# Ordering TensorE's queue by hand in an Infini-attention plus SiLU kernel: an emission clock, held-back dependent work, w1 products spread over the score tiles

## The chip, the cores and the metric

The kernel runs on one core of one Trainium2 chip. The metric is device time in microseconds (us), lower is better. Engines are named as the profile names them: PE is the matrix engine (TensorE), ACT the scalar engine, DVE the vector engine, POOL the GpSimd engine, SP the queue that issues most DMAs.

## The reference, cut to what matters

```python
xn  = layernorm(x)                       # x: 2048 rows x 512
out = x + attention(xn) + mlp(xn)

# attention: 32 heads of 16, four segments of 512 rows, one after another
q, k, v = xn @ wq, xn @ wk, xn @ wv
for s in range(4):
    p     = softmax(qs @ ks.T / 4 + causal_mask)
    a_dot = p @ vs
    a_mem = (phi(qs) @ M) / (phi(qs) @ z + 1e-6)
    o_s   = g * a_mem + (1 - g) * a_dot          # g = sigmoid(beta), per head
    M, z  = M + phi(ks).T @ vs, z + sum(phi(ks)) # phi(t) = t + 1 if t > 0 else exp(t)
attention = concat(o_s) @ wo

# mlp: 512 -> 1792 -> 512
mlp = silu(xn @ w1) @ w2
```

## The kernel before

The work of a segment is cut into 20 score tiles. A score tile is four or eight small matmuls into four PSUM banks, one exp of 128x2048 on ACT, and a causal mask on POOL. All else on PE is "filler" put between score tiles: the next segment's projections, PV and Z (the softmax's denominators), the memory matrix (`psM`), normalisation (`psR`, `psD`, `psN`), 14 w1 products per segment (`ps`, then tanh on ACT, a product on DVE, giving one `hT` tile), and four output rows per segment with 14 w2 and 4 wo matmuls each. All fillers share three PSUM banks (`pp`), but for Z, which adds up in a bank of its own.

The program's text fixes the order only roughly. The scheduler of the framework, which works with a model of durations, orders every engine's queue, PE's too. The main loop hands out fillers by a budget:

```python
    def fillers(s):
        # ... (segment 0: rest of the projections, layernorm of segment 1)
        if s > 0 and s < 3:
            yield from mem_fill(s, sts[s], sts[s + 1])
        if s < 3:
            # ...
            yield from proj_fill(s + 1, sts[s + 1])
        if s > 0:
            yield from out_fill(s - 1, sts[s - 1])   # normalise, w2, wo of the last segment
        yield from h_some(s, FT)                     # 14 w1 products in a row
        # ...

            for quad in range(5):
                s_quad(st, dt, quad, tiles)          # scores, exp, mask
                budget += STEP_BUDGET                # 2300
                # ...
                while budget > 0:
                    c = next(fill, None)
                    if c is None:
                        break
                    budget -= c
```

One w1 product shows the dependent chain that matters: PE, then ACT, then DVE, and only then is the PSUM bank free again (the page of the kernel before puts 4.7 us of PE's waits at this line on that DVE product).

```python
            ps = gemm4(...)                                           # PE, 4 matmuls
            nc.scalar.activation(out=th[:], in_=ps[:, :], func=AF.Tanh)
            nc.vector.scalar_tensor_tensor(                           # (tanh + 1) * ps
                out=hT[:], in0=th[:], scalar=1.0, in1=ps[:, :], op0=ALU.add, op1=ALU.mult)
```

Tanh gives silu because w1 is scaled by 0.5 first, which is a job of POOL in the head of the program.

The softmax here doesn't subtract the row's maximum and nothing guards it: scores larger than these inputs give would overflow.

Of the kernel before, what the change touches and what calls it, by code (L numbers as in the profile page):

```python
# [1 line left out]

# [9 lines left out]
F32 = mybir.dt.float32  # L12

P = 128
# [13 lines left out]
STEP_BUDGET = 2300  # L28
# [3 lines left out]
def kernel(  # L32
# [20 lines left out]
    hpool = ctx.enter_context(tc.tile_pool(name="hpool", bufs=20))  # L53
# [4 lines left out]
    psatt = ctx.enter_context(tc.tile_pool(name="psatt", bufs=1, space=bass.MemoryType.PSUM))  # L58


    beta_b = cpool.tile([P, H], BF16, name="beta_b")
    nc.gpsimd.dma_start(
        out=beta_b[:], in_=bass.AP(tensor=A_beta.tensor, offset=A_beta.offset, ap=[[0, P], [1, H]])
    )
# [6 lines left out]

    xts = {}

    def load_x(s, half, eng):
        xt = xpool.tile([P, 2, D], BF16, name="x_in")
        r0 = s * L + half * 256
        eng.dma_start(
            out=xt[:], in_=x_flat[r0 : r0 + 256, :].rearrange("(two p) d -> p two d", p=P)
        )
        xts[(s, 2 * half)] = xt[:, 0, :]  # L80
        xts[(s, 2 * half + 1)] = xt[:, 1, :]

    load_x(0, 0, nc.sync)
    load_x(0, 1, nc.scalar)
    nc.sync.dma_start(out=wk_sb[:], in_=A_wk.rearrange("(ko ki) n -> ki ko n", ki=P))
    nc.scalar.dma_start(out=wq_sb[:], in_=A_wq.rearrange("(ko ki) n -> ki ko n", ki=P))
    nc.sync.dma_start(out=wv_sb[:], in_=A_wv.rearrange("(ko ki) n -> ki ko n", ki=P))
    nc.sync.dma_start(out=w1_sb[:], in_=B_w1.rearrange("(ko ki) n -> ki ko n", ki=P))
    nc.sync.dma_start(out=wo_sb[:], in_=A_wo.rearrange("(ko ki) n -> ki ko n", ki=P))
    nc.sync.dma_start(out=w2_sb[:], in_=B_w2.rearrange("(ko ki) n -> ki ko n", ki=P))  # L90
    load_x(1, 0, nc.scalar)
    load_x(1, 1, nc.sync)

# [3 lines left out]

# [7 lines left out]
    oneh = cpool.tile([P, 8, 32], BF16, name="oneh")  # L105
    nc.gpsimd.memset(oneh[:], 0.0)
    for i in range(8):
        nc.gpsimd.memset(oneh[:, i, i : i + 1], 1.0)


    zbias = cpool.tile([P, 1], F32, name="zbias")
    nc.gpsimd.memset(zbias[:], 1.0)
    for g in range(4):
        nc.gpsimd.memset(zbias[32 * g : 32 * g + 16, :], 1e-6)
        nc.gpsimd.memset(zbias[32 * g : 32 * g + 8, :], 0.0)


    smask = cpool.tile([P, H], F32, name="smask")
    nc.gpsimd.memset(smask[:], 0.0)
    for base, val in ((0, -1.0), (8, 1.0)):  # L120
        for dt in range(DT):
            v = smask[:, 8 * dt : 8 * dt + 8].rearrange("p (b c) -> p b c", b=4)
            nc.gpsimd.affine_select(
                out=v, in_=v, compare_op=ALU.not_equal, fill=val, base=-(base + 2 * dt),
                pattern=[[-32, 4], [-1, 2]], channel_multiplier=1,
            )
    gt = cpool.tile([P, H], F32, name="gt")
    gcol = cpool.tile([P, 1], F32, name="gcol")
    nc.vector.tensor_tensor(out=gt[:], in0=smask[:], in1=beta_b[:], op=ALU.mult)
    nc.vector.reduce_sum(out=gcol[:], in_=gt[:], axis=mybir.AxisListType.X)  # L130
    nc.scalar.activation(out=gcol[:], in_=gcol[:], func=AF.Tanh, scale=0.5)
    nc.vector.tensor_scalar(
        out=gcol[:], in0=gcol[:], scalar1=0.5, scalar2=0.5, op0=ALU.mult, op1=ALU.add
    )
    selb = cpool.tile([P, 2, DT, 8], F32, name="selb")
    nc.gpsimd.memset(selb[:], 0.0)
    for w, base in ((0, 0), (1, 8)):
        for dt in range(DT):
            v = selb[:, w, dt, :].rearrange("p (a b) -> p a b", a=4)
            nc.gpsimd.affine_select(  # L140
                out=v, in_=v, compare_op=ALU.not_equal, fill=1.0, base=-(base + 2 * dt),
                pattern=[[-32, 4], [-1, 2]], channel_multiplier=1,
            )
    sel = cpool.tile([P, 2, DT, P], BF16, name="sel")
    nc.vector.tensor_scalar(
        out=sel[:, :, :, :].rearrange("p w t (h d) -> p (w t h) d", d=DH),
        in0=selb[:, :, :, :].rearrange("p w t h -> p (w t h)").unsqueeze(2).broadcast_to([P, 64, DH]),
        scalar1=gcol[:, 0:1], scalar2=None, op0=ALU.mult,
    )


    bmask = cpool.tile([P, P], BF16, name="bmask")
    zmask = cpool.tile([P, DT, P], BF16, name="zmask")
    nc.gpsimd.memset(bmask[:], 1.0)
    nc.gpsimd.memset(zmask[:], 0.0)
    bm_v = bmask[:, :].rearrange("p (a b) -> p a b", a=8)
    for v in [bm_v]:
        nc.gpsimd.affine_select(
            out=v, in_=v, compare_op=ALU.is_ge, fill=0.0, base=0,
            pattern=[[-16, 8], [0, 16]], channel_multiplier=1,  # L160
        )
        nc.gpsimd.affine_select(
            out=v, in_=v, compare_op=ALU.is_ge, fill=0.0, base=15,
            pattern=[[16, 8], [0, 16]], channel_multiplier=-1,
        )
    for dt in range(DT):
        zv = zmask[:, dt, :].rearrange("p (g r) -> p g r", g=4)[:, :, 8 + 2 * dt : 10 + 2 * dt]
        nc.gpsimd.tensor_copy(
            out=zv, in_=bm_v[:, :, 0].rearrange("p (g r) -> p g r", g=4)
        )  # L170
# [6 lines left out]
    lnc = cpool.tile([P, TPS, 2], F32, name="lnc")  # L177
    nc.gpsimd.memset(lnc[:, :, 0:1], EPS)
    nc.gpsimd.memset(lnc[:, :, 1:2], -0.5)

    def ln_stats(s):
        for j in range(TPS):
            t = s * TPS + j
            stats = work.tile([P, nc.vector.BN_STATS_DIM], F32, name="stats")
            nc.vector.bn_stats(out=stats[:], in_=xts[(s, j)])
            nc.vector.bn_aggr(out=mv_all[:, t, :], in_=stats[:])
        rs = rstd_all[:, s * TPS : (s + 1) * TPS, :]
        nc.gpsimd.tensor_tensor(
            out=rs, in0=mv_all[:, s * TPS : (s + 1) * TPS, 1:2], in1=lnc[:, :, 0:1], op=ALU.add
        )  # L190
        nc.gpsimd.tensor_tensor(out=rs, in0=rs, in1=lnc[:, :, 1:2], op=ALU.pow)

    def ln_tile(s, j):
        t = s * TPS + j
        xn_t = work.tile([P, D], BF16, name="xn_t")
        nc.vector.tensor_scalar(  # L196
            out=xn_t[:], in0=xts[(s, j)],
            scalar1=mv_all[:, t, 0:1], scalar2=rstd_all[:, t, 0:1],
            op0=ALU.subtract, op1=ALU.mult,
        )  # L200
        ptr = pp.tile([P, 4, P], BF16, name="ptr", tag="ps")
        for dt in range(DT):
            nc.tensor.transpose(ptr[:, dt, :], xn_t[:, dt * P : (dt + 1) * P], ident[:])  # L203
        nc.vector.tensor_copy(out=xnT[s][:, :, j * P : (j + 1) * P], in_=ptr[:, :, :])

    def ln_fill(s):
        ln_stats(s)
        xnT[s] = segp.tile([P, DT, L], BF16, name="xnT")
        yield 0
        for j in range(TPS):  # L210
            ln_tile(s, j)
            yield 280


    def gemm4(lhsTs, rhss):
        ps = pp.tile([P, L], F32, name="ps", tag="ps")
        for ki in range(DT):
            nc.tensor.matmul(  # L218
                ps[:, :], lhsT=lhsTs(ki), rhs=rhss(ki), start=(ki == 0), stop=(ki == DT - 1)
            )  # L220
        return ps

    def phi_part(ps, dst, acc=None):
        ek = work.tile([P, L], BF16, name="ek", bufs=2)
        nc.scalar.activation(out=ek[:], in_=ps[:, :], func=AF.Exp)  # L225
        nc.gpsimd.tensor_scalar(  # L226
            out=ek[:], in0=ek[:], scalar1=1.0, scalar2=0.0, op0=ALU.min, op1=ALU.max
        )
        nc.vector.scalar_tensor_tensor(  # L229
            out=dst, in0=ps[:, :], scalar=0.0, in1=ek[:], op0=ALU.max, op1=ALU.add, accum_out=acc  # L230
        )

    vts = []
    for i in range(2):
        vt = cpool.tile([P, TPS, H // 2, 3, DH], BF16, name=f"V{i}")
        nc.gpsimd.memset(vt[:, :, :, 1, :], 0.0)
        vts.append(vt)

    def proj_fill(s, st):
        kT = segp.tile([P, DT, L], BF16, name="kT")  # L240
        kTo = segp.tile([P, DT, L], BF16, name="kTo")
        qT = segp.tile([P, DT, L], BF16, name="qT")
        V = vts[s % 2]
        st.update(kT=kT, kTo=kTo, qT=qT, V=V)
        if s < NSEG - 1:
            phiK = segp.tile([P, TPS, D], BF16, name="phiK", bufs=1)
            zc = segp.tile([P, DT], F32, name="zc")
            st.update(phiK=phiK, zc=zc)
        if s > 0:
            phiQT = segp.tile([P, DT, L], BF16, name="phiQT", bufs=3)  # L250
            st["phiQT"] = phiQT

        pend = []

        def k_transposes(dt, phiKT):
# [107 lines left out]
    def out_fill(s, st):  # L363
        while "rec" not in st:
            yield None
# [256 lines left out]
```

## Time and profile before

The kernel before takes 353.62 us (median of three runs, 351.61 to 354.32). The profiled execution has a span of 349.9 us.

| what | before |
|---|---|
| first scores on PE | 24.0 us |
| exp of the first / 80th score tile starts | 25.1 / 309.4 us |
| mean distance of two exps | 3.60 us |
| from the 80th exp's start to the end | 40.5 us |

These lines of the profile's page of the kernel before give the busy time of each engine, then PE's busy share and the granted PE clock in 40 slices of the span (a digit is tenths; 9 is 90% or more):

```profile
PE 276.9 (79%) x2416; PEld 120.5 (34%) x2452; DVE 176.4 (50%) x308; ACT 195.0 (56%) x166; POOL 131.7 (38%) x251
...
PE   0388868898987899998799789978589997642696
...
PEclk9999999999997899999999999999959999755599
```

No engine is full. PE is nearest, and at the end of the program (slices 35 to 38) it is both half idle and at half clock. The same page has the largest group of ACT, the exps: after the bar stand their busy time and mean duration in ns, then how long ACT was idle just before them and for whom it waited.

```profile
L446 ACT ACTIVATE Pt<-psS 128x2048 bf16<-128x2048 f32 x80 | 150.2, 1877 | 70.2 <-PE psS L439 69.8
```

ACT waited 70 us in all for score tiles: exps do not follow one another every 1.88 us, PE's order decides when each may start. The next view is the windows view of the kernel before. A line is a stretch, its length, then the busy time of PE, PE's weight loads, DVE, ACT and POOL in it, the granted clock, DMA share and GB/s. The first three are head, body and tail.

```profile
0.00:24.02 24.02, 8.30 (x32) 3.48 (x33) 11.18 (x30) 2.68 (x4) 18.65 (x69) 1.00 0.96 305
24.02:309.40 285.38, 243.73 (x2262) 106.60 (x2297) 150.75 (x262) 189.75 (x160) 111.47 (x182) 0.96 0.05 15
309.40:349.90 40.50, 24.85 (x122) 10.42 (x123) 14.52 (x18) 2.56 (x2) 1.60 (x2) 0.71 0.06 20
...
40.00:60.00 20.00, 15.42 (x141) 7.23 (x147) 17.32 (x43) 10.44 (x12) 14.14 (x28) 1.00 0.08 27
310.00:320.00 10.00, 3.34 (x41) 1.88 (x42) 4.04 (x2) 1.96 (x2) 1.09 (x1) 0.50 0.00 0
```

The body has 41.6 us without PE work, the tail 15.7, the head 15.7. (Some matmul records are missing from this trace: PE has 2416 beside 2452 weight loads, so busy times of PE are a little low. The tail's 122 should be 124.) Last, the timeline of the kernel before in its head; a line is start, duration, engine, source line, operation, and in brackets how long the engine was idle before it and what released it.

```profile
8.94 1.29 DVE L185 BATCH_NORM_STATS2 stats<-x_in 128x6 f32<-128x512 bf16 x2 [3.00 <-DMA x_in<-in_A_x_dram]
...
16.63 1.87 PE L218 MATMUL ps<-xnT,wk_sb 128*128 128x512 bf16 x4 [0.51 <-DVE xnT L204]
...
24.02 0.39 PE L439 MATMUL psS<-qT,kTo 32*128 32x512 bf16 x3 [1.51 <-POOL kTo L270]
```

The second half of x lands late, the first products are slow (1.87 us for four matmuls, against 1.04 later; the windows view shows a clock of 1.00 for the head only because the profile has no clock record before 21.2 us), and the first scores wait for POOL (1.51 us). Below, "cold" is a granted clock of 0.50 and "warm" one of 1.00.

### The profile page before, as it was taken

The page shows a single profiled execution, that of the slowest core. Times are in us where ns is not written, and L with a number is a line of the kernel's source. Part 1 is how long each engine was busy: PE and PEld are TensorE (multiplying, and loading weights), DVE is VectorE, ACT ScalarE, POOL GpSimd, SP SyncE. Part 2 cuts the span into 40 slices and gives each one's busy share as a digit, 9 for nine tenths or more (in the row PEclk, how much of TensorE's full clock was granted, in tenths as well). Part 3 has the DMA queues.
Part 4 walks back from the last instruction along what each step waited for, and adds up shares of the span by engine and source line. Part 5 has one row for each costly group of instructions (what it writes and reads, how often), then busy time and mean ns, then how long its engine had stood idle before and what let it go on. Part 6 is the DMA issues. An engine that isn't in the chain of part 4 may idle for free.

```text
span 349.9 us, 5880 instructions
## 1 busy us (share of the span) xinstructions
PE 276.9 (79%) x2416; PEld 120.5 (34%) x2452; DVE 176.4 (50%) x308; ACT 195.0 (56%) x166; POOL 131.7 (38%) x251
## 2 busy tenths in 40 slices
PE   0388868898987899998799789978589997642696
PEld 0233423343342434443343334433224443320242
DVE  1749987457457661126878641235661234007511
ACT  1026265697988646779648627588740679640000
POOL 8587477333265733333246313231220233330000
PEclk9999999999997899999999999999959999755599
DMA  7980100000000000110000001110000110000011
GB/s 203 383 256 3 60 32 0 0 2 3 0 2 2 0 3 30 34 61 0 2 0 3 0 19 43 32 32 0 2 0 30 47 48 0 2 0 0 2 49 41
DMA packets 11290, 12.44 MB, mean 36 GB/s; under 512 B 752, under 2 KB 10752, under 8 KB 11264
## 3 DMA queue, kind: packets, MB, share of 16 engines
q1 hardware_dynamic: 10160, 11.01, 9.8%
q10 hardware_dynamic: 1072, 1.05, 0.9%
q8 instruction: 19, 0.31, 0.3%
q0 software_dynamic: 32, 0.01, 0.3%
q14 instruction: 7, 0.06, 0.1%
HBM read 9.97 MB, written 2.10 MB: 34 GB/s over the span
## 4 chain that ended last, share of the span: by engine, by line
PE 43%; DVE 22%; ACT 15%; POOL 9%; issue 6%; DMA 4%; SPq 0%; POOLq 0%; ACTq 0%
PE psO L404 13%; ACT Pt L446 10%; PE ps L218 9%; DVE hT L315 5%; ACT th L313 4%; PE psPV L477 4%; PE psS L439 4%; DMA w_sb<-in_B_w_dram 4%; DVE rec L507 4%; PE psO L411 4%; PE psZ L488 3%; POOL Pt L455 3%; DVE pq L382 2%; POOL w_sb L516 2%; PE psN L391 2%
## 5 line engine op out<-in xcount | busy, mean ns | idle before, releaser
L446 ACT ACTIVATE Pt<-psS 128x2048 bf16<-128x2048 f32 x80 | 150.2, 1877 | 70.2 <-PE psS L439 69.8
L455 POOL TENSOR_SCALAR_AFFINE_SELECT Pt<-Pt 128x512 bf16<-128x512 bf16 (+1 forms) x112 | 76.9, 700 | 160.3 <-ACT Pt L446 160.3
L218 PE MATMUL ps<-xnT,w_sb 128*128 128x512 bf16 x213 | 52.8, 379 | 5.4 <-DVE hT L315 4.7
L315 DVE SCALAR_TENSOR_TENSOR hT<-th,ps 128x512 bf16<-128x512 bf16 x56 | 37.0, 684 | 38.2 <-ACT th L313 36.9
L404 PE MATMUL psO<-w_sb,hT 128*128 128x512 bf16 x212 | 53.2, 388 | 1.2 <-issue 0.8
L416 DVE TENSOR_TENSOR o_t<-psO,x_res 128x512 bf16<-128x512 f32 x16 | 11.1, 692 | 54.4 <-PE psO L411 54.4
L313 ACT ACTIVATE th<-ps 128x512 bf16<-128x512 f32 x56 | 32.1, 606 | 8.2 <-PE ps L218 5.2
L404 PEld LDWEIGHTS <-hT 128*128 128x128 bf16 x224 | 21.1, 100 | 29.5 <-issue 8.6
L218 PEld LDWEIGHTS <-w_sb 128*128 128x128 bf16 x224 | 20.3, 97 | 30.4 <-issue 10.7
L488 PE MATMUL psZ<-Pt,oneh 128*32 128x128 bf16 (+3 forms) x512 | 29.3, 323 | 1.6 <-POOL Pt L455 1.2
L225 ACT ACTIVATE ek<-ps 128x512 bf16<-128x512 f32 x24 | 14.2, 598 | 27.2 <-DVE kT L265 14.4
L483 DVE CAST N_sb<-psPV 128x512 bf16<-128x512 f32 x16 | 11.0, 688 | 29.3 <-PE psPV L477 29.2
L439 PE MATMUL psS<-qT,kTo 32*128 32x512 bf16 (+3 forms) x256 | 19.6, 310 | 6.7 <-ACT Pt L446 5.0
L439 PE MATMUL psS<-qT,kT 16*128 16x512 bf16 (+3 forms) x256 | 20.3, 314 | 5.7 <-ACT Pt L446 5.4
L218 PE MATMUL ps<-xnT,wk_sb 128*128 128x512 bf16 x58 | 18.6, 428 | 2.7 <-DVE phiKT L229 0.7
L203 PE MATMUL ptr<-ident,xn_t 128*128 128x128 bf16 x64 | 7.0, 241 | 17.2 <-DVE xn_t L196 16.4
L218 PE MATMUL ps<-xnT,wq_sb 128*128 128x512 bf16 x62 | 17.9, 412 | 2.9 <-DVE phiKT L229 2.8
L488 PEld LDWEIGHTS <-oneh 128*32 128x32 bf16 x512 | 13.9, 101 | 14.9 <-issue 9.9
L218 PE MATMUL ps<-wv_sb,xnT 128*128 128x512 bf16 x61 | 15.7, 379 | 3.3 <-DVE phiQT L229 2.0
L477 PE MATMUL psPV<-Pt,V_212 128*32 128x384 bf16 (+3 forms) x256 | 12.9, 327 | 4.7 <-POOL Pt L455 4.7
L411 PE MATMUL psO<-wo_sb,oT 128*128 128x512 bf16 x64 | 16.4, 379 | 0.0
L226 POOL TENSOR_SCALAR ek<-ek 128x512 bf16<-128x512 bf16 x24 | 14.6, 615 | 2.4 <-ACT ek L225 2.3
(85 smaller groups left out, 286.3 us busy)
## 6 DMA issues: line engine op xcount, KB each, us to landing
w_sb<-in_B_w_dram SPq DMA_DIRECT2D x2, 1792.0 KB, 15.4
x_res<-in_A_x_dram SPq DMA_DIRECT2D x16, 128.0 KB, 2.2
out_dram<-o_t SPq DMA_DIRECT2D x16, 128.0 KB, 1.7
x_in<-in_A_x_dram SPq DMA_DIRECT2D x6, 256.0 KB, 3.1
wq_sb<-in_A_wq_dram ACTq DMA_DIRECT2D x1, 512.0 KB, 4.9
wk_sb<-in_A_wk_dram SPq DMA_DIRECT2D x1, 512.0 KB, 7.9
x_in<-in_A_x_dram ACTq DMA_DIRECT2D x2, 256.0 KB, 8.0
wv_sb<-in_A_wv_dram SPq DMA_DIRECT2D x1, 512.0 KB, 9.4
```

The lines of the kernel that those rows point to most:

```text
L218: nc.tensor.matmul(ps[:, :], lhsT=lhsTs(ki), rhs=rhss(ki), start=(ki == 0), stop=(ki == DT - 1))
L225: nc.scalar.activation(out=ek[:], in_=ps[:, :], func=AF.Exp)
L226: nc.gpsimd.tensor_scalar(out=ek[:], in0=ek[:], scalar1=1.0, scalar2=0.0, op0=ALU.min, op1=ALU.max)
L313: nc.scalar.activation(out=th[:], in_=ps[:, :], func=AF.Tanh)
L315: nc.vector.scalar_tensor_tensor(out=hT[:], in0=th[:], scalar=1.0, in1=ps[:, :], op0=ALU.add, op1=ALU.mult)
L404: nc.tensor.matmul(psO[:, :], lhsT=st["hT"][ft][:, j * P : (j + 1) * P], rhs=w2_sb[:, ft, :], start=(ft == 0), stop=False,)
L411: nc.tensor.matmul(psO[:, :], lhsT=oT[:, dt, j * P : (j + 1) * P], rhs=wo_sb[:, dt, :], start=False, stop=(dt == DT - 1),)
L439: nc.tensor.matmul(psS[:, g, c : c + nq], lhsT=kk[r0:r1, dt, kt * P : (kt + 1) * P], rhs=st["qT"][r0:r1, dt, kt * P : L], start=True, stop ...
L446: nc.scalar.activation(out=Pt[:], in_=psS[:], func=AF.Exp, scale=SCALE)
L455: nc.gpsimd.affine_select(out=v, in_=v, compare_op=ALU.is_ge, fill=0.0, base=0, pattern=[[0, v.shape[1]], [1, P]], channel_multiplier=-1,)
L477: nc.tensor.matmul(o_ap, lhsT=lhsT, rhs=p_view(tiles, par, g, kt), start=(par == 1 and kt == 0), stop=(par == 0 and kt == kts[-1]), tile_p ...
L488: nc.tensor.matmul(psZ[32 * g : 32 * g + 32, kt * P : L], lhsT=oneh[:, 2 * dt + par, :], rhs=p_view(tiles, par, g, kt), start=(first and p ...
```

## The change

PE's queue is taken out of the scheduler's hands. The program counts a clock while it emits instructions: `pe(ns)` adds the time PE should need, and `later(ns, fn)` holds an instruction back until that much PE time has been emitted after its input. Each score tile gets 2000 ns of filler and, once its own segment's projections are done, one w1 product if the ring of 23 hT tiles has room. x is loaded first, weights and constants after it, 44 dummy matmuls run ahead of everything else on PE, meant to warm the array, kTo of segment 0 comes straight from PSUM. The w2 products of the last segment go into the four score banks while that segment is normalised.

```diff
+    ctx.enter_context(tc.manual_schedule(engines={ENG.PE}))
 ...
+    def run_due():
+        while held and held[0][0] <= clock["vt"]:
+            heapq.heappop(held)[2]()
+
+    def pe(ns):
+        clock["vt"] += ns
+        run_due()
+
+    def later(ns, fn):
+        clock["n"] += 1
+        heapq.heappush(held, (clock["vt"] + ns, clock["n"], fn))
 ...  (all of h_fill is new; its end:)
+                later(700, glu)
+                yield True
 ...  (normalisation: psN is held back behind the DVE products)
+                later(1700, lambda dt=dt, a_t=a_t, pq=pq: fin(dt, a_t, pq))
 ...  (head)
+    for i in range(WARM):
+        nc.tensor.matmul(warm[:, :], lhsT=ident[:], rhs=ident[:], start=True, stop=True)
 ...  (main loop)
+                end = clock["vt"] + 430 + FILL_NS
                 s_quad(st, dt, quad, tiles)
-                budget += STEP_BUDGET
 ...
+                if st.get("ready"):
+                    pull(hgen)
 ...
+                while clock["vt"] < end:
+                    moved = None
+                    if not due_done:
+                        moved = pull(due)
 ...  (then output rows of the segment before, then w1 products)
+                    if not moved:
+                        clock["vt"] = min([end] + [h[0] for h in held[:1]])
+                        run_due()
 ...  (tail)
+    psO4 = psatt.tile([P, 4, L], F32, name="psO4", tag="psS")
+    nf = norm_fill(s, st)
+    for j in range(TPS):
+        for f0 in range(0, FT, 4):
+            w2_part(st, j, psO4[:, j, :], range(f0, min(FT, f0 + 4)))
+            pull(nf)
```

Some smaller parts of the change are not in this cut. The function phi is computed from the copies of k and q in SBUF and no longer from the PSUM bank, so that a projection's bank is free after its copies. The statistics are taken per half of x, ACT makes some of the copies in the head, and the ring of hT tiles grows from 20 to 23. In the kernel before, PE waited 6.4 us in sum for banks that phi held (4.4 for `phiKT`, 2.0 for `phiQT`).

## The prediction

> **What bounds the kernel now.** The busy table gives PE 276.9 us of a 349.9 us span, ACT 195.0, DVE 176.4, POOL 131.7. No engine is full: order and latency bound it, with PE nearest. By the group and timeline durations with a warm array PE needs less: a four-matmul product 0.86 us (104 in projections and w1, 16 in wo), w2 3.0 us per row tile (16), scores 0.43 us per score tile (80), PV and Z 1.2 us each (16 each), the rest about 23. Sum about 248 us. The span's remainder:
>
> - Head: the timeline shows the first projection at 16.6 us, the first scores at 24.0. The second x half lands at 8.9 us, products run at 427 ns per matmul until 21.3 us, and kTo waits on POOL behind 6.6 us of w1 scaling.
> - Body: windows show PE 15.4 of 20 us busy at 40 to 60 us with DVE at 17.3. w1 products in a row advance one per 1.83 us (tanh, DVE product, exp), though PE needs 0.86.
> - Tail: fillers run out. From 300 to 330 us PE is busy 13.4 of 30 us at clock 0.50 to 0.67; after the last PV/Z (315 us) come reciprocal 3.35 us, serial normalisation to 329, then w2/wo of the last segment (16 us) alone.
>
> [...]
>
> **What the change does.** It fixes PE's order by a clock counting 430 ns of scores plus 2000 ns of filler per score tile, adds dependent work only when its input should be ready, and gives every score tile one w1 product, so exp (1.88) plus tanh (0.6) hides under PE work. Head: x first on one queue, constants and w1 scaling later, kTo direct from PSUM, 44 warm-up matmuls. Tail: last w2 runs in the score banks during normalisation.
>
> **Cost.** PE arithmetic is unchanged. Head: first scores near 14 us (-10). Body: with 0.86 us pieces a step overshoots 2.43 to about 2.84 us, and 80 of them consume just the filler that exists. I expect 3.15 us: three PSUM banks serve all fillers (a w1 bank is held about 4 us, a projection's 2.4, so about 2.9 a step), DVE has about 54 us of work in segment 0's 57, and each 3.35 us reciprocal blocks the drains. 80 x 3.15 = 252 against 285 now (24.0 to 309.4). Tail: PV/Z 2.6, w2 12, wo 3.4, with waits 22, last add and store 3.5: about 26 against 40. Sum 14 + 252 + 26 = 292 us; timed runs lie up to 2 us above the span: **292 us, 277 to 312**. Faster by over 2%: 0.96; same 0.03; slower 0.01.
>
> **What would show it.** PE busy about 255 us (no cold stretches), over 85% of the span; clock about 1.0 after 10 us; first scores by 15 us; mean exp spacing about 3.1 us; no three tanh in a row; last w2 done before normalisation ends; tail after the last scores under 30 us. PE waits left: on DVE drains of filler banks.
>
> **What would make it wrong.** A fixed queue blocks at its head: if engines lag the emission clock, each mistimed product stops scores too (3.5 us a step, over 310). If banks and DVE cost nothing, 2.9 us a step, about 272.

In the trace the granted clock of the kernel before is 0.50 from 110 to 117, 253 to 264, 298 to 301 and 305 to 332 us from the span's start; a four-matmul product takes 1.86 us at 111.75 us, where the clock is 0.50, and 1.04 us at 120.14, where it is 1.00.

That 44 matmuls would warm the array, and that PE would then have no cold stretches (255 us): read both as estimates. Estimates too are the bank holds (4 and 2.4 us) and the 54 us of DVE work in the body's term; in the trace of the kernel after DVE is busy for 52.6 of the 67.2 us from the first scores to the 21st exp. For the two blocks that it names, the traces below give a size in single places: scores 4.9 us after the last ones behind products that waited 0.78 us for DVE (at 102 us, under e_auto), and a 2.03 us wait of PE for a DVE product behind a reciprocal (at 288 us, in the tail).

## The result, and the profile after

The changed kernel is correct and takes 318.55 us (median of four runs, 315.41 to 320.09) against 353.43 (351.61 to 354.32) for the kernel before in the same rounds. The ratio is 0.901 (95% interval 0.893 to 0.909). Ratios here are the mean time of one kernel's runs over that of the other's of the same rounds, so they are not quite the ratio of the medians quoted. Executions over 1.5% slower than the fastest of the same kernel are left out of the means. The change is worth 10%, but the forecast of 292 us was too low by 26.6 us, and 318.55 lies outside its range.

The page of the kernel after, the same three lines and the group of the exps:

```profile
PE 265.2 (84%) x2496; PEld 117.2 (37%) x2496; DVE 179.7 (57%) x306; ACT 198.0 (63%) x172; POOL 137.0 (43%) x254
...
PE   5277869999977887899987889899989799997993
...
PEclk9589999999999799999997999999999999997999
...
L466 ACT ACTIVATE Pt<-psS 128x2048 bf16<-128x2048 f32 x80 | 150.1, 1876 | 57.4 <-PE psS L458 54.0
```

The half-empty end is gone, the clock is close to full after the third slice, and ACT waits 54 us for scores in place of 70. The windows view of the kernel after, with head, body and tail cut at its own first scores and its own 80th exp:

```profile
0.00:21.35 21.35, 9.04 (x68) 6.53 (x69) 11.72 (x22) 3.67 (x5) 16.32 (x68) 0.76 0.94 315
21.35:276.37 255.02, 224.27 (x2239) 96.76 (x2239) 148.48 (x259) 188.76 (x161) 118.98 (x186) 0.99 0.06 17
276.37:316.00 39.63, 31.91 (x190) 13.89 (x188) 19.49 (x26) 5.55 (x7) 1.66 (x2) 0.96 0.11 34
```

| term of the sum | before | forecast | after |
|---|---|---|---|
| head: to the first scores | 24.0 | 14 | 21.35 |
| body: to the 80th exp | 285.4 | 252 | 255.0 |
| tail | 40.5 | 26 | 39.6 |
| sum | 349.9 | 292 | 316.0 |

The body came nearly as forecast. Head and tail did not: 7.4 and 13.6 us over. The timeline of the kernel after shows what happened in the head:

```profile
2.38 4.01 PE L552 MATMUL warm<-ident 128*128 128x128 bf16 x44 [2.38 <-POOL ident masks.py:199]
...
11.59 0.69 DVE L132 BATCH_NORM_STATS2 stats<-x_in 128x6 f32<-128x512 bf16 x1 [5.05 <-DMA x_in<-in_A_x_dram]
...
13.07 1.03 PE L155 MATMUL ptr<-ident,xn_t 128*128 128x128 bf16 x8 [6.69 <-DVE xn_t L143]
...
16.52 6.71 POOL L570 TENSOR_SCALAR w_sb<-w_sb 128x1792 bf16<-128x1792 bf16 x4
16.59 3.46 DVE L143 TENSOR_SCALAR xn_t<-x_in,mv_all,rstd_all 128x512 bf16<-128x512 bf16 x2 [0.48 <-POOL rstd_all L138]
...
21.35 0.40 PE L458 MATMUL psS<-qT,kTo 32*128 32x512 bf16 x4 [1.64 <-DVE qT L259]
21.68 1.04 PE L180 MATMUL ps<-xnT,wk_sb 128*128 128x512 bf16 x4
```

DVE had the statistics of segment 0 done at 6.5 us, and POOL the factors from them at 9.0. But DVE stood idle for 5.05 us and normalised segment 0 only at 12.2, because the scheduler had put the statistics of segment 1 (line 132 at 11.59) ahead of that in DVE's queue, and their data came at 11.6 us. (With that one entry moved, in e_head below, the same normalisation starts at 8.35 us.) Later, two normalisations of segment 1 (16.59) sit in front of the kTo and qT copies, and take 1.73 us each while POOL scales w1 in pieces of 1.68 to 1.72 us; the same operation takes 0.40 us in the head of the kernel before, ahead of the scaling there, and 0.51 us in e_headw2, which does not scale w1. By what means POOL slows DVE is not shown.

The timeline of the tail of the kernel after, from the 80th exp at 276.37:

```profile
277.06 3.19 PE L401 MATMUL psO<-w_sb,hT 128*128 128x512 bf16 x14
...
281.04 1.27 PE L500 MATMUL psPV<-Pt,V_121 128*32 128x512 bf16 x32
...
283.33 2.76 PE L180 MATMUL ps<-xnT,w_sb 128*128 128x512 bf16 x12
...
288.12 3.13 PE L180 MATMUL ps<-xnT,w_sb 128*128 128x512 bf16 x8 [2.03 <-DVE hT L301]
291.04 1.51 PE L401 MATMUL psO_3943<-w_sb,hT 128*128 128x512 bf16 x4
...
302.75 3.62 PE L401 MATMUL psO_3943<-w_sb,hT 128*128 128x512 bf16 x16
...
306.21 1.03 PE L410 MATMUL psO_3943<-wo_sb,oT 128*128 128x512 bf16 x4
308.01 1.02 PE L410 MATMUL psO_3943<-wo_sb,oT 128*128 128x512 bf16 x4 [0.78 <-DVE o_t L416]
```

Before the w2 products of the last segment (291.04), the tail does work that belongs to the body: the wo products of one output row of segment 2 and the whole of the last (276.2 to 281.0, 4.85 us) and five w1 products (283.3 to 291.0, 7.7 us, of which 2.0 waiting for a DVE product that stands behind the 3.35 us reciprocal). These 42 matmuls (22 and 20) come on top of the 148 that the last segment needs after its last scores and make the 190 of this tail. (The tail before had 124 of the 148: 24 of its PV and Z matmuls ran before the 80th exp.) So the tail was freed of its cold and idle time (clock 0.96 against 0.71, 7.7 us without PE work against 15.7), and the room was filled by left-over filler: the length stayed.

### The profile page after: what moved, and what is told of

Read it like the earlier page. It is cut to its first block, busy times and chain, and to the rows that moved or that the text cites. A ratio compares the mean times of both kernels' runs of the same rounds, so it can differ in the third digit from the quotient of the medians.

```text
span 316.0 us, 6029 instructions
## 1 busy us (share of the span) xinstructions
PE 265.2 (84%) x2496; PEld 117.2 (37%) x2496; DVE 179.7 (57%) x306; ACT 198.0 (63%) x172; POOL 137.0 (43%) x254
## 4 chain that ended last, share of the span: by engine, by line
PE 56%; DVE 22%; POOL 9%; issue 5%; ACT 5%; DMA 1%; POOLq 0%; ACTq 0%
PE ps L180 15%; PE psO L401 12%; PE psS L458 6%; PE psZ L519 5%; PE psO_3943 L401 4%; PE psPV L500 4%; DVE hT L301 4%; PE psO L410 3%; ACT Pt L466 2%; ACT th L295 2%; POOL w_sb L570 2%; DVE rec L541 2%; DVE stats L132 2%; DVE phiKT L197 2%; DVE phiQT L197 2%
## 5 line engine op out<-in xcount | busy, mean ns | idle before, releaser
L466 ACT ACTIVATE Pt<-psS 128x2048 bf16<-128x2048 f32 x80 | 150.1, 1876 | 57.4 <-PE psS L458 54.0
L180 PE MATMUL ps<-xnT,w_sb 128*128 128x512 bf16 x224 | 57.9, 391 | 8.1 <-DVE hT L301 7.5
L401 PE MATMUL psO<-w_sb,hT 128*128 128x512 bf16 x168 | 41.9, 383 | 0.0
L458 PE MATMUL psS<-qT,kTo 32*128 32x512 bf16 (+3 forms) x256 | 17.7, 308 | 4.3 <-ACT Pt L466 2.6
L416 DVE TENSOR_TENSOR o_t<-psO,x_res 128x512 bf16<-128x512 f32 x12 | 8.2, 685 | 21.9 <-PE psO L410 21.9
L519 PE MATMUL psZ<-Pt,oneh 128*32 128x128 bf16 (+3 forms) x512 | 20.3, 300 | 0.0
L458 PE MATMUL psS<-qT,kT 16*128 16x512 bf16 (+3 forms) x256 | 17.1, 300 | 1.1 <-ACT Pt L466 1.1
L191 POOL TENSOR_SCALAR ek<-ek 128x512 bf16<-128x512 bf16 x24 | 15.5, 651 | 4.1 <-ACT ek L188 4.1
L155 PE MATMUL ptr<-ident,xn_t 128*128 128x128 bf16 x64 | 6.9, 248 | 11.3 <-DVE xn_t L143 10.2
L541 DVE RECIPROCAL rec<-zf 128x512 bf16<-128x512 f32 x4 | 13.4, 3351 | 4.5 <-ACT zf L536 4.5
L132 DVE BATCH_NORM_STATS2 stats<-x_in 128x6 f32<-128x512 bf16 x16 | 10.4, 678 | 9.6 <-DMA x_in<-in_A_x_dram 9.3
L519 PEld LDWEIGHTS <-oneh 128*32 128x32 bf16 x512 | 11.5, 96 | 10.3 <-issue 5.0
L458 PEld LDWEIGHTS <-kTo 32*128 32x128 bf16 x256 | 5.4, 92 | 22.4 <-issue 20.2
## 6 DMA issues: line engine op xcount, KB each, us to landing
wo_sb<-in_A_wo_dram SPq DMA_DIRECT2D x1, 512.0 KB, 12.1
```

The costliest lines, as they stand in the source:

```text
L132: nc.vector.bn_stats(out=stats[:], in_=xts[(s, 2 * half + j)])
L180: nc.tensor.matmul(ps[:, :], lhsT=lhsTs(ki), rhs=rhss(ki), start=(ki == 0), stop=(ki == DT - 1))
L191: nc.gpsimd.tensor_scalar(out=ek[:], in0=ek[:], scalar1=1.0, scalar2=0.0, op0=ALU.min, op1=ALU.max)
L401: nc.tensor.matmul(psO, lhsT=st["hT"][ft][:, j * P : (j + 1) * P], rhs=w2_sb[:, ft, :], start=(ft == 0), stop=False,)
L458: nc.tensor.matmul(psS[:, g, c : c + nq], lhsT=kk[r0:r1, dt, kt * P : (kt + 1) * P], rhs=st["qT"][r0:r1, dt, kt * P : L], start=True, stop ...
L466: nc.scalar.activation(out=Pt[:], in_=psS[:], func=AF.Exp, scale=SCALE)
```

## The experiments

Three questions: does the missing gain lie in the head, in the tail, or in the fixed order itself? And which part of the change brought the 10%? The theory on reading the trace was: (a) the head is lost to one entry out of place in DVE's queue; (b) the tail is lost to left-over filler; (c) holds and spreading carry the gain. The rivals: the fixed order itself costs or gives the most, or DVE's amount of work, not its order, bounds segment 0.

All 18 variants compute correct results. The table has all of them; times are medians of four runs (six for the last), each beside the kernel before on the same chip. The starts of exps are of the profiled run; "11th" and "21st" say how much of a gain in the head was still there in segment 0 and at its end.

| label | time, us | ratio to before | first / 11th / 21st exp | tail |
|---|---|---|---|---|
| (after) | 318.55 | 0.901 | 21.8 / 57.4 / 88.5 | 39.6 |
| e_head | 318.05 | 0.902 | 16.1 / 57.6 / 88.7 | 39.6 |
| e_headw2 | 317.32 | 0.902 | 19.8 / 55.7 / 86.8 | 39.6 |
| e_head3 | 323.76 | 0.913 | 16.1 / 61.4 / 92.5 | 39.6 |
| e_head4 | 318.58 | 0.900 | 17.2 / 53.0 / 86.8 | 39.8 |
| e_head5 | 311.03 | 0.875 | 16.5 / 52.6 / 83.7 | 39.8 |
| e_nowarm | 322.22 | 0.915 | 22.2 / 60.8 / 92.2 | 39.7 |
| e_nohold | 359.25 | 1.022 | 26.0 / 75.1 / 114.9 | 39.5 |
| e_nospread | 346.86 | 0.986 | 22.1 / 67.3 / 106.7 | 29.8 |
| e_fill2300 | 336.31 | 0.952 | 22.1 / 59.5 / 91.8 | 31.4 |
| e_oldtail | 320.50 | 0.911 | 22.2 / 59.0 / 90.1 | 43.1 |
| e_tail2 | 318.53 | 0.901 | 22.3 / 57.5 / 88.6 | 38.8 |
| e_auto | 309.01 | 0.877 | 22.2 / 58.8 / 89.6 | 36.4 |
| a_nohold | 332.35 | 0.939 | 22.1 / 65.7 / 103.1 | 36.4 |
| a_nospread | 331.23 | 0.935 | 21.8 / 56.9 / 97.9 | 28.7 |
| a_head3 | 310.60 | 0.878 | 16.9 / 61.3 / 92.1 | 36.4 |
| a_head4 | 305.52 | 0.862 | 17.8 / 53.6 / 86.6 | 36.6 |
| a_all3 | 317.51 | 0.896 | 15.7 / 63.4 / 94.3 | 37.9 |
| a_head5 | 300.18 | 0.847 | 15.5 / 48.3 / 79.9 | 36.6 |

### The head: e_head

The statistics of segment 1 are tied behind the last normalisation of segment 0 (an ordering hint to the scheduler, no data moves):

```diff
-        ln_stats(s, 0)
-        ln_stats(s, 1)
+        with tc.issue_after(norm_ins[(0, TPS - 1)]):
+            ln_stats(s, 0)
+            ln_stats(s, 1)
```

> The changed kernel, with the layer-norm statistics of segment 1 tied to come after the last normalisation of segment 0 on DVE. Theory 1 (the head gained nothing because DVE sat at the segment 1 statistics, whose x landed at 11.6 us, while rstd of segment 0 was ready at 9.0 us): first normalisation near 9.1 us instead of 12.2, first scores about 3 to 4 us earlier (17.5 to 18.5 instead of 21.4), whole time 3 to 4 us less than the changed kernel, so about 315. Rival (the head is bound by the arrival of the weights or by the cold array): first scores stay at 20 to 21 us and the time is unchanged.

The first scores came at 15.7 us in place of 21.35, nearly at the forecast of the prediction. The time did not move: 0.902 against 0.901, and the 11th exp starts at 57.6 us as before the edit. Theory (a) is right about the first block, and wrong that the first scores are worth their 5.7 us. The timeline of e_head shows the next block:

```profile
24.11 1.86 PE L184 MATMUL ps<-xnT,wq_sb 128*128 128x512 bf16 x4 [5.00 <-DVE qT L263]
```

PE stood 5.0 us, went cold (1.86 us for four matmuls; the granted clock is 0.50 from 24.1 to 27.4 us), and had lost all that was won. DVE had been idle for 7.1 us before its product `phiKT` at 22.76, which waited for a POOL operation behind the 6.63 us of w1 scaling.

### The head, one block after another: e_headw2, e_head3, e_head4, e_head5

e_headw2 is e_head with the w1 scaling taken away: tanh takes the factor 0.5 itself, and POOL halves w2 instead, in one piece of 512 columns per score tile.

```diff
-                nc.scalar.activation(out=th[:], in_=ps[:, :], func=AF.Tanh)
+                nc.scalar.activation(out=th[:], in_=ps[:, :], func=AF.Tanh, scale=0.5)
 ...
-    for kc in range(DT):
-        nc.gpsimd.tensor_scalar(
-            out=w1_sb[:, kc, :], in0=w1_sb[:, kc, :], scalar1=0.5, scalar2=1.0,
 ...
+                kc = 5 * dt + quad - 5
+                if s == 0 and 0 <= kc < FT:
+                    nc.gpsimd.tensor_scalar(
+                        out=w2_sb[:, kc, :], in0=w2_sb[:, kc, :], scalar1=0.5, scalar2=1.0,
```

> The run with the statistics tied behind the normalisation, and w1 no longer scaled on POOL at the start: tanh takes scale 0.5 and w2 is halved later, one piece per score tile. That run had its first scores at 15.7 us but gave the 5.7 us back by 57 us, PE waiting 5.0 us for qT at 24 us. Theory (it was given back because POOL is in the 6.7 us w1 scaling until 23 us, and DVE behind it): the 5 us stay, 312 to 315 us, exp number 11 at about 52 us instead of 57.6. Rival (the segment 0 stage is bound by DVE work, and an earlier start only fills the wait): exp number 11 still at 56 us or later, time above 316.

It gained nothing that can be told from e_head (0.902). Its timeline has a new block, the normalisations of segment 1, which wait in DVE's queue for their own statistics:

```profile
16.83 1.02 DVE L143 TENSOR_SCALAR xn_t<-x_in,mv_all,rstd_all 128x512 bf16<-128x512 bf16 x2 [4.13 <-POOL rstd_all L138]
```

The first scores stood behind it (they start at 19.16, having waited 3.54 us for qT). Two normalisations beside no scaling of w1 took 1.02 us, not 3.46.

e_head3 ties statistics and normalisations of segment 1 behind the third qT copy of segment 0:

```diff
-        ln_stats(s, 0)
-        ln_stats(s, 1)
+        with tc.issue_after(q_ins[(0, 2)]):
+            ln_stats(s, 0)
+            ln_stats(s, 1)
 ...
+            if j < TPS:
+                with tc.issue_after(q_ins[(0, 2)]):
+                    prev = ln_norm(s, j)
```

> The fixed PE order, w1 not scaled at the start, and statistics and normalisation of segment 1 tied on DVE behind the third qT copy of segment 0. In the run before it DVE still stood 4.1 us (12.2 to 16.8 us) at a normalisation of segment 1 whose rstd POOL had not made. Theory (the head is a chain of DVE head-of-line blocks, three of which are now gone): first scores near 15.7 us, second exp 3 to 4 us later, exp number 11 at 50 to 53 us instead of 57.4, time 4 to 6 us less than the changed kernel, 312 to 315. Rival (segment 0 is bound by the DVE work itself, about 54 us): exp number 11 at 55 us or later, exp number 21 at 87 us or later, time 316 or more.

It is if anything slower than after, 323.76 us (the two intervals to the kernel before overlap a little). The timeline of e_head3:

```profile
22.47 1.21 POOL L687 TENSOR_SCALAR w_sb<-w_sb 128x512 bf16<-128x512 bf16 x2 [3.84 <-DMA w_sb<-in_B_w_dram]
...
23.35 0.36 DVE L606 TENSOR_TENSOR gt<-smask,beta_b 128x32 f32<-128x32 f32 x1 [4.13 <-DMA beta_b<-in_A_beta_dram]
```

Two more blocks of the same kind. The gate's first product waited for beta, whose DMA the change had moved from first place to the end of the queue; and the first w2 piece on POOL waited for w2. Neither is work that anything needs so early.

e_head4 loads beta first (on POOL's DMA queue, as in the kernel before), ties the gate behind the first qT copy, and starts the w2 pieces one score tile later, tied behind a mask.

```diff
+    beta_b = cpool.tile([P, H], BF16, name="beta_b")
+    nc.gpsimd.dma_start(
 ...
+    with tc.issue_after(q_ins[(0, 0)]):
+        nc.vector.tensor_tensor(out=gt[:], in0=smask[:], in1=beta_b[:], op=ALU.mult)
 ...
+                kc = 5 * dt + quad - 6
+                if s == 0 and 0 <= kc < FT:
+                    with tc.issue_after(mask_ins[-1]):
```

> The fixed PE order with the head's last blocks taken away: beta loaded first (DVE stood 4.1 us, to 23.4 us, at the gate column whose beta came last), w2 halved only from score tile 6 on, each piece tied on POOL behind a mask (POOL stood 3.8 us, to 22.5 us, at w2's arrival), segment 1's normalisation tied as before. Theory (every early start so far was given back at the next head-of-line block on DVE or POOL, and now none is left): exp number 1 near 17 us, exp number 11 at 50 to 53 us instead of 57.4, time 312 to 315 us. Rival (segment 0 is bound by its DVE work, about 30 us in each 35): exp number 11 at 55 us or later, time 317 or more.

Now the 11th exp is at 53.0 us, 4.3 us before that of after: the gain of the head survived its first blocks. By the 21st exp 1.7 us are left, and the total is that of after (318.58). Two theories were open for that: segment 0 is bound by the amount of work on DVE, so that nothing won before it lasts; or the w2 pieces, moved from the head into segment 0, take it back on POOL, where the masks must pass.

e_head5 tells them apart. It scales nothing at all: tanh takes 0.5, `sel` is doubled, and the last addition becomes `0.5 * psO + x`. The gate is tied behind the fourth qT copy.

```diff
-        nc.vector.tensor_tensor(out=o_t[:], in0=psO, in1=x_t[:], op=ALU.add)
+        nc.vector.scalar_tensor_tensor(
+            out=o_t[:], in0=psO, scalar=0.5, in1=x_t[:], op0=ALU.mult, op1=ALU.add
+        )
 ...
-        scalar1=gcol[:, 0:1], scalar2=None, op0=ALU.mult,
+            scalar1=gcol[:, 0:1], scalar2=2.0, op0=ALU.mult, op1=ALU.mult,
```

> The fixed PE order with the head cleared and nothing put in its place: tanh takes scale 0.5, the factor two goes into the gate matrix and a half into the last addition, so neither w1 nor w2 is scaled on POOL (in the run before POOL had 9.3 us of w2 pieces in score tiles 6 to 19, where the 4.4 us won by the eleventh were lost again). Theory (the head's gain survives if POOL gets no new work): exp number 11 at 50 to 54 us and exp number 21 at 82 to 85 us against 88.5, time 312 to 315. Rival (DVE work bounds segment 0): exp number 21 at 86 us or later, time 317 or more.

The gain lasted: 21st exp at 83.7 us (after: 88.5), total 311.03 us (308.86 to 311.35), 7.5 us below after. Of these, 4.8 us are there at the 21st exp; where the rest was won was not traced. The windows view of the same stretch of segment 0, 50 to 85 us, first in e_head4 and then in e_head5:

```profile
50.00:85.00 35.00, 31.43 (x305) 13.72 (x304) 24.11 (x41) 29.85 (x31) 28.04 (x43) 1.00 0.01 2
```

```profile
50.00:85.00 35.00, 33.67 (x317) 14.45 (x316) 24.38 (x43) 31.96 (x34) 22.20 (x32) 1.00 0.01 2
```

DVE is as busy in both (24.1 and 24.4 of 35 us), so its amount of work is not the bound. POOL differs by 5.8 us, and PE did 2.2 us more where POOL did less. The rival on DVE's work fell. The gate was moved as well, but at the 11th exp the two runs are still equal within 0.5 us (53.0 and 52.6), and the 3.1 us between them come after it, so the gate is not the reason.

### The head's warm-up: e_nowarm

```diff
-WARM = 44
+WARM = 0
```

> The changed kernel without the 44 warm-up matmuls. Theory (they ended at 6.4 us and the first real matmul came at 13.1, so the array had cooled: the first products still took 427 ns a matmul): no change beyond noise, 316 to 320 us. Rival (they do buy something): 2 us or more slower.

Without the dummy matmuls the kernel takes 322.22 us, 3.7 more than after, a ratio of 1.016 between the two (the intervals to the kernel before, 0.910 to 0.921 and 0.893 to 0.909, just miss each other). In the kernel after, the burst ends at 6.4 us and PE then idles until 13.07; the granted clock is 1.00 from 5.3 us, where its record begins, to 8.7, and 0.50 from there to 18.9. The first product is as slow in both (1.87 us for four matmuls, at 16.75 in after and at 15.11 in e_nowarm). The difference is the third one: in after it takes 1.04 us (line 180 at 21.68 above), and in the timeline of e_nowarm

```profile
21.57 0.62 PE L458 MATMUL psS<-qT,kTo 32*128 32x512 bf16 x4 [3.39 <-DVE qT L259]
22.11 1.89 PE L180 MATMUL ps<-xnT,wk_sb 128*128 128x512 bf16 x4
```

it is cold still (the granted clock is 0.50 from 21.0 to 24.3 us, and 1.00 in after). But the first products of e_nowarm came 1.6 us sooner while DVE did not, so PE had just waited 3.39 us for qT, against 1.64 in after. That wait is a rival for the cold product, so a use of the burst is not shown. No run here separates the two.

### What carries the gain: e_nohold and e_nospread

e_nohold sets all hold times to zero, so that dependent work is emitted as soon as its input is:

```diff
-        heapq.heappush(held, (clock["vt"] + ns, clock["n"], fn))
+        heapq.heappush(held, (clock["vt"] + 0.0 * ns, clock["n"], fn))
```

> The changed kernel with every hold of dependent work set to zero (transposes of phi, products of the normalisation, masks, w1 drains follow at once), PE order still fixed. Theory (a fixed queue blocks at its head, so the holds are what makes a fixed order bearable): 8% or more slower, above 340 us. Rival (the engines lag the emission clock so far that the holds do little): within 2%.

e_nospread makes the w1 products five in a row, at every fifth score tile, in place of one per tile:

```diff
-                if st.get("ready"):
-                    pull(hgen)
+                if st.get("ready") and quad == 4:
+                    for _ in range(5):
+                        pull(hgen)
```

> The changed kernel with the w1 products pulled five at a time at the fifth score tile of each group, in place of one per score tile. Theory (w1 in a row is bound by tanh, DVE product and exp at 1.83 us a product): 6 to 12 us slower. Rival (the hT ring of 23 is full during 36 of the 60 score tiles of segments 1 to 3 anyhow, so little is spread in the changed kernel either): within 3 us.

(Both needed two small guards so that the emission could not run into itself; the guards alone were not run.) Without holds the kernel takes 359.25 us, 40.7 more than after and more than the kernel before: a fixed PE order whose dependent work comes too early is worse than the scheduler's order. Without the spread it takes 346.86 us, 28.3 more; the body is 40.2 us longer and the tail 9.8 us shorter. That is far above the 6 to 12 us of the expectation, so the size of the effect is not explained by its theory. So each of the two is needed for most of the whole gain of 35 us. A rival for the second was that spreading hardly happens: the ring of 23 hT tiles is full for long, and in a count made while the program is emitted, 36 of the 60 score tiles of segments 1 to 3 get no w1 product. The spread was worth 28 us all the same, so this rival fell. A larger ring was not run.

### The fixed order itself: e_auto, a_nohold, a_nospread

e_auto takes one line away. The program emits in the same order, with the same holds, but the scheduler orders PE's queue, as in the kernel before.

```diff
-    ctx.enter_context(tc.manual_schedule(engines={ENG.PE}))
```

> The changed kernel without the hand-made PE order: the emission order is only a priority and the scheduler orders PE as before. Theory (the fixed PE order is what lowers the time per score tile from 3.6 to 3.2 us): 335 to 350 us, mean exp spacing 3.4 us or more. Rival (what pays is the new emission itself, the tail and the holds, and the fixed order matters little): 312 to 322 us.

It is faster than the change: 309.01 us (308.32 to 310.60) against 318.55, a ratio of 0.974. The order by hand costs 9.5 us. The windows view of e_auto, cut as above, without the head:

```profile
21.41:270.73 249.32, 227.58 (x2200) 97.68 (x2234) 148.99 (x259) 188.59 (x160) 118.97 (x186) 0.99 0.06 17
270.73:307.10 36.37, 30.28 (x187) 13.43 (x188) 19.24 (x26) 5.55 (x7) 1.67 (x2) 1.00 0.12 37
```

The body is 5.7 us shorter than in after, the tail 3.3. The timeline of PE in the kernel after, at one place where exps lie 5.1 us apart:

```profile
102.11 0.40 PE L458 MATMUL psS<-qT,kTo 32*128 32x512 bf16 x4 [2.04 <-ACT Pt L466]
...
103.60 0.38 PE L384 MATMUL psR<-rec,sel 128*128 128x512 bf16 x1 [0.56 <-DVE oT L387]
104.20 0.53 PE L384 MATMUL psR<-rec,sel 128*128 128x512 bf16 x1 [0.22 <-DVE oT L387]
104.80 2.26 PE L327 MATMUL psM<-V_121,phiK 128*128 128x128 bf16 x16
106.99 0.61 PE L458 MATMUL psS<-qT,kTo 32*128 32x384 bf16 x8
```

and the same place in e_auto:

```profile
102.20 0.38 PE L409 MATMUL psO<-wo_sb,oT 128*128 128x512 bf16 x1
...
102.89 0.40 PE L457 MATMUL psS<-qT,kTo 32*128 32x512 bf16 x4
103.22 0.40 PE L326 MATMUL psM<-V,phiK 128*128 128x128 bf16 x4
...
104.09 0.50 PE L518 MATMUL psZ<-Pt,oneh 128*32 128x256 bf16 x5
...
105.63 0.40 PE L457 MATMUL psS<-qT,kTo 32*128 32x384 bf16 x8
```

In the first, the next scores stand behind the whole of `psR` and `psM`, and `psR` waits for DVE twice (0.56 and 0.22 us). In the second, pieces of `psZ`, `psO` and `psM` fill the gaps and the next scores come 2.7 us after the last. So in after what stood ahead in PE's queue held the scores behind it: they came 4.9 us after the last ones, with 0.78 us of waits and 2.26 us of `psM` in between.

With the scheduler on PE, holds and spread were then taken away once more, with the edits above:

> PE left to the scheduler and all holds zero. Theory (the holds repair what the fixed PE order breaks, so without a fixed order they do nothing): within 5 us of the scheduler's 309.0. Rival (the holds also order DVE, ACT and POOL and keep filler banks free): 15 us slower or more, against 40 us with the fixed order.

> PE left to the scheduler and w1 products five at a time at every fifth score tile. Theory (spreading works on the ACT and DVE chain of w1, which the scheduler's PE order can't shorten): 15 to 30 us slower than 309.0, as with the fixed order (28). Rival (five products in a row only block the scores of a fixed queue): within 5 us of 309.0.

a_nohold takes 332.35 us and a_nospread 331.23, that is 23.3 and 22.2 us over e_auto. Both parts of the change work in any case, holds more so where the order is fixed (40.7 us), probably because there nothing else can repair a bad place. So the gain of the change over the kernel before comes in the main from what is emitted when, and the fixing of the order gives some of it back.

### The tail: e_oldtail, e_tail2, e_fill2300

e_oldtail normalises first and then does the w2 and wo products in filler banks, as the kernel before did:

```diff
-    psO4 = psatt.tile([P, 4, L], F32, name="psO4", tag="psS")
     nf = norm_fill(s, st)
-    for j in range(TPS):
-        for f0 in range(0, FT, 4):
-            w2_part(st, j, psO4[:, j, :], range(f0, min(FT, f0 + 4)))
-            pull(nf)
     while pull(nf) is not None or held:
 ...
+    for _ in out_fill(s, st):
+        pass
```

> The changed kernel with the last segment's w2 products put back behind its normalisation, in the filler banks, as before the change. Theory (the score banks hide 12 us of w2 behind reciprocal and normalisation, which take about 15 us): 7 to 11 us slower than the changed kernel, about 326 to 330. Rival (the normalisation is only slowed by sharing PE, and nothing is hidden): within 3 us of it.

320.50 us, ratio 0.911 (0.905 to 0.918) to the kernel before; the tail is 3.5 us longer, and the whole kernel 1% slower than after with overlapping intervals, so unclear. Hiding w2 under the normalisation is worth some 3 us of the tail, far from what the forecast of the tail counted on. One reason is in the two traces: the normalisation alone takes 8.9 us in e_oldtail (290.5 to 299.4), and 11.3 us with w2 products between its steps in after (292.4 to 303.6), since each step now also stands behind a block of w2 in PE's queue.

e_tail2 moves the left-over w1 products behind the w2 products that are already possible, so that they run during the normalisation:

```diff
-    while pull(hgen):
-        pass
 ...
+    have = st["nh"] - st["nh"] % 4
+    for j in range(TPS):
+        for f0 in range(0, have, 4):
+            w2_part(st, j, psO4[:, j, :], range(f0, f0 + 4))
+            pull(nf)
+    while pull(hgen):
+        pull(nf)
 ...  (then the rest of the w2 products)
```

> The changed kernel with the tail's order alone changed: the w2 products whose w1 products exist (eight of fourteen per row tile) run right after the last Z, under the reciprocal, and the five w1 products left over come after them. Theory (the tail's 39.6 us hold a 2.0 us wait at the reciprocal and 3.4 us at half clock because the left-over w1 products come at the wrong place): tail 3 to 5 us shorter, 313 to 316 us. Rival (the tail is bound by its PE work and the serial normalisation): within 1.5 us of the changed kernel.

318.53 us, tail 38.8: nothing that can be told from after. This order of the tail is not the matter; the next run tests whether the amount of work is.

e_fill2300 gives each score tile 2300 ns of filler in place of 2000, so that less is left over:

```diff
-FILL_NS = 2000
+FILL_NS = 2300
```

> The changed kernel with 2300 ns instead of 2000 ns of filler after each score tile. Theory 2 (13.6 us too much in the tail is filler that the 80 score tiles left over, about 9 us of PE work done badly, with the clock at half and DVE in the reciprocal): fewer w1 and w2 products after the last scores, tail shorter by 5 to 9 us, body longer by 3 to 7, time 2 to 5 us less. Rival (the body is bound by something else than its filler, so more filler only stretches it): body longer by as much as the tail is shorter, time within 1 us or longer.

The tail fell to 31.4 us as it should, but the exps moved apart from 3.22 to 3.54 us and the kernel took 336.31 (334.80 to 337.65 in the three fast executions, 339.94 in the slow one). So left-over filler is the cause of the tail's length (e_nospread and a_nospread agree: with nothing left over, 148 weight loads, their tails take 29.8 and 28.7 us), and pushing it back into the body costs more there than it saves here. Why the body lost 25 us for 8 us of work was not traced further; twelve of its steps are over 4.5 us, against six in after.

### Putting things together: a_head3, a_all3, a_head4, a_head5

These are e_head3, e_head4 and e_head5 with the scheduler on PE (the e_auto edit). a_all3 adds to a_head3 the tail of e_tail2, a reciprocal in four pieces and 80 dummy matmuls.

> The same head as the first run of this call, but PE left to the scheduler. Theory (the fixed order costs 9 us whatever the head): 8 to 10 us less than that run, and 4 to 6 us less than the run with the scheduler's PE order and the old head (309.0), so 303 to 305. Rival (the scheduler's PE order hid the head's blocks, so the gains don't add): 308 or more.

> As the third run, with the tail of the second, 80 warm-up matmuls, and the reciprocal in four pieces of 0.85 us between which DVE can drain filler banks. Theory (each 3.35 us reciprocal blocks the drains of the filler banks, as the prediction had it): 3 to 8 us less than the third run, 296 to 301. Rival (the scheduler's PE order fills those waits with PV and Z products already): within 2 us of the third run.

> The same head with PE left to the scheduler. Theory: the gains add, 302 to 306 us against 309.0 with the old head. Rival: 308 or more.

> The same with PE left to the scheduler, the best version the runs point to: 299 to 304 us if the head's gain survives, 305 or more if not (305.5 with w2 scaled on POOL).

a_head3, 310.60 us, keeps the blocks of e_head3 and gains nothing over e_auto. a_all3, 317.51 us, was worse than a_head3: its second exp came 12.1 us after its first, with PE waiting 7.9 us for qT. It mixes three edits with those blocks, so it says nothing about the split reciprocal (the 0.85 us a piece is an estimate, a quarter of the 3.35 us of the whole one). a_head4 takes 305.52 us. a_head5, free of blocks and of scaling, takes 300.18 us (299.27 to 303.26, six runs), ratio 0.847 to the kernel before (0.841 to 0.854). It beats both kernels. Its windows, cut as above:

```profile
0.00:14.67 14.67, 9.44 (x74) 6.99 (x74) 6.49 (x16) 3.99 (x6) 10.69 (x60) 1.00 0.84 278
14.67:261.03 246.36, 227.73 (x2234) 96.83 (x2234) 149.77 (x265) 188.69 (x160) 119.09 (x191) 1.00 0.09 29
261.03:297.60 36.57, 30.44 (x190) 13.46 (x188) 19.24 (x26) 5.55 (x7) 1.67 (x2) 0.98 0.12 36
```

Head, body and tail are 6.7, 8.7 and 3.1 us shorter than in the kernel after. PE's body is 18.6 us from being full; in after it was 30.7. Against e_head5 the scheduler on PE is worth 10.9 us, as it was worth 9.5 between after and e_auto. The tail still has all its 190 matmuls: the left-over filler may be the largest thing still to be won, but no run here found room for it in the body.

## Why the prediction was right or wrong

- **Direction.** Right: faster by over 2%. The size was not: 318.55 us measured, 292 forecast, range 277 to 312.
- **"First scores near 14 us (-10)".** Mis-sized, 21.35 us measured. The prediction freed PE, POOL and the DMAs, and did not ask what stands in DVE's queue, which the scheduler orders. e_head showed that one misplaced entry held the first scores for 5.7 us. It also showed that the first scores are the wrong measure: the blocks behind it (POOL's w1 scaling, normalisations of segment 1, beta, w2) each took the gain back. With all of them gone (e_head5) the first scores came at 16.0 us, 5.4 earlier than in after, and the total fell by 7.5 us. That this is the size by which the term was over (7.4) is partly chance, as only 4.8 us of it were there at the 21st exp.
- **"80 x 3.15 = 252".** Nearly right: 255.0 us, 3.22 between exps. But not for the reason given, so the near hit is partly luck. "80 of them consume just the filler that exists" is wrong: 42 matmuls were left over, so the body was that much easier than assumed, and it still took 3 us longer. The fixed order is enough to fill that difference. The prediction named that risk ("a fixed queue blocks at its head"), and gave it no term in the sum; e_auto and the pair e_head5 and a_head5 measured it at 9.5 to 10.9 us of total time, of which 5.7 lies in the body of e_auto (249.3 us against 255.0, both from the first scores to the 80th exp).
- **"Tail: about 26 against 40".** Mis-sized, 39.6. The items of the sum were PV/Z 2.6 (2.3 measured), w2 12 (15.2 together with the normalisation that it hides), wo 3.4 (6.5, of which 2.3 are three waits of 0.78 us for the addition that reads the shared tile), last add and store 3.5 (3.3). The step that failed is the missing item: 12.6 us of left-over output rows and w1 products, 4.85 and 7.7. The ring of 23 hT tiles is why w1 products are left: while it is full none can be made.
- **"PE busy about 255 us", "over 85%".** Measured 265.2 and 84%. A cold clock is not the reason: a_head5, at a mean clock of 0.997, has 267.6. So the list of warm durations (248 us) was itself too short, by some 15 us beside the 4 us of dummy matmuls. A single matmul is shown with 0.38 us (`psR` at 103.60 in after) while one in a row adds 0.22 (line 180 from 21.68 in after), so a queue cut into many pieces shows more busy time; how much that makes in sum was not separated.
- **Signs that were right.** The clock is near full in the body (0.99). PE's waits left are on DVE: hT 7.5 us, qT 3.5 us. **Wrong ones:** the last w2 product ends at 306.4, after the normalisation (303.6), and five tanh follow one another in the tail.

In one sum: head 7.4, body 3.0 and tail 13.6 us over the forecast make the 24 us between 292 and the span of 316.0. The steps that failed are the path of the head (it runs through DVE's queue, which the prediction left out) and the claim that 80 score tiles consume all filler (42 matmuls, 12.6 us, were left to the tail).

## What to carry to other kernels

Hold dependent work back and spread chains that cross engines, one link per step of the main loop: here that carried the gain under either order of PE's queue. Then try the same emission with the scheduler's order before you keep one made by hand, and check the DVE and POOL queues for entries that wait on a late DMA before work that is urgent; clear all of them before you judge, since clearing one only shows the next, and don't pay for a cleared head with work moved into the busy body. When you forecast a tail, count what the body leaves over: shortening the body without finding room for its filler moves work to the end, it does not remove it.
